# A kernel with its order written out: warm-up matmuls that read the rows of tiles 1 to 3, tile 0 ahead of the others, and a new order on every engine

## The chip, the cores and the metric

The kernel runs on one core of a Trainium2 chip. The core has four compute engines that run side by side: TensorE (PE; its weight loads, PEld, overlap its matmuls), VectorE (DVE), ScalarE (ACT) and GpSimd (POOL), and SyncE (SP), whose queue issues most transfers. Each engine works through its own queue in order and waits on semaphores for the others. The metric is the time of one execution on the device in microseconds (us), as the median of several runs.

## The reference

Inputs are `A_q`, `A_k`, `A_v` of 2048 rows by 640 channels, a short filter, a long filter per channel, and three weight matrices. All are bf16.

```python
xn = _layernorm(A_q)                       # per row, over 640 channels
# branch A: a short filter over 4 rows of k, times v, then a causal convolution with 2048 taps per channel
kv = k_shift * v                           # k_shift[n] = sum over t < 4 of k[n - t] * shift_k[:, t]
y  = irfft(rfft(kv, 4096) * rfft(ssm_k, 4096))[:2048] + kv * ssm_D
A  = xn * y
# branch B: a gated linear unit
g = xn @ w_gate; u = xn @ w_up             # 640 -> 1728
B = (sigmoid(g) * u) @ w_down              # 1728 -> 640
out = A_q + A + B
```

## The kernel before

The 2048 rows lie in 16 tiles of 128 rows, in one buffer `acc` that also collects the output. Four tiles make a group (`tr` 0 to 3).

For branch B, a group is normalised (`rec_stat`, `rec_fast` or `rec_rsq`, `rec_norm`), transposed into `xnT` (group 0 by TensorE and PSUM in `rec_tp`, the others by a transposing transfer), and projected in 14 chunks of 128 columns: five matmuls of 128x512 each for the gate and for the up projection (`rec_fc`, line 774). ScalarE takes the sigmoid (line 736), VectorE multiplies it with the up projection (line 738) into `hT`. Then `rec_down` (line 790) multiplies `hT` with `w_down` in two halves of seven matmuls for each output tile and half of its columns, and VectorE adds the result to `acc` (line 801). The last tile is cut into columns of 320, 240 and 80. Projections and down projections share two PSUM accumulators of one bank (tag `g`).

The first two chunks of group 0 are computed tile by tile as the tiles become ready (`rec_first`, line 753, narrow matmuls of 128x128 and 128x256 into PSUM tiles `c0_0` and `c0_1`), so that work can start before all four tiles are there.

Branch A replaces the convolution by matmuls with tables in ten steps (`idx` 0 to 9). `rec_kv` makes the short filter and its product with v on VectorE (lines 484 to 491, into `kvt`), `rec_st1` (line 510), `rec_st2` (line 530) and `rec_st3` (line 578) are the stages on TensorE, `rec_prod` (lines 552 to 564) the spectral product on VectorE, and `rec_st4` (line 610) the last stage, whose result is multiplied with xn and added to `acc`. Stage results leave PSUM through ScalarE or VectorE (`ev`, lines 329 to 333).

At the start, TensorE runs nine matmuls of zeros on the tile `warm` (line 819, planned at line 820) and, behind the normalised tile 0, one more (line 849). Their result in `wps` is never read.

```python
    for m0, m1 in ((0, 1), (1, 4)):
        for q in range(4):
            load_x(q, m0, m1, "ACT" if q > 1 else "SP", FIX)
```

These loads bring tile 0 and tiles 1 to 3, each in four pieces of 32 partitions, on two queues.

Nothing is scheduled at run time. Each call of `plan.op` records an operation with what it reads and writes. The list `ORDER` (line 79) names the recorded operations by number in the order in which they are emitted, and so fixes the order on every engine and in every queue. `ON_DVE` names the PSUM evacuations that VectorE takes; ScalarE takes the others. The figures for durations and for transfers (`few` in `load_x`) are for a planner that made `ORDER`; they are not used when the kernel is built.

Of the kernel before, what the change touches and what calls it, by code (L numbers as in the profile page):

```python
# [44 lines left out]
def _dft_tables():  # L45
# [31 lines left out]


ORDER = [
# [38 lines left out]
]  # L118
ON_DVE = [
    98, 102, 104, 139, 140, 142, 147, 148, 195, 248, 380, 397, 424, 445, 446, 470, 480, 486, 498, 504, 605  # L120
]


# [94 lines left out]
def kernel(  # L218
# [146 lines left out]

    def load_x(q, m0, m1, eng, pri):
        dma(lambda e: e.dma_start(acc[32 * q:32 * q + 32, m0:m1, :], xq4[q][:, m0:m1, :]), 32, 1280 * (m1 - m0), q=eng,
            few=1.0 if m0 == 0 else 1.2 if m0 == 1 else 2.4, w=[("acc", m, q) for m in range(m0, m1)], pri=pri)

    def weight(tr, n):  # L370
        tr = 0 if tr == 1 else tr
# [264 lines left out]
    def rec_stat(m, pri):  # L636
        b = f"bs{m}"
        ak = [("acc", m, q) for q in range(4)]
        for s2 in range(2):
            dve(320, 1, lambda s2=s2: nc.vector.bn_stats(tl[b][:, 6 * s2:6 * s2 + 6], acc[:, m, s2 * 320:(s2 + 1) * 320]),  # L640
                r=ak, w=[(b, s2)], alloc=[(b, "bs")] if s2 == 0 else (), pri=pri)
        dve(8, 1, lambda: nc.vector.bn_aggr(st[:, 0:2, m], tl[b].rearrange("p (a c) -> p a c", a=2)),
            r=[(b, 0), (b, 1)], w=[("mv", m)], pri=pri)

# [71 lines left out]
    def rec_evac(tr, fc, cs, pri):  # L716
        two = isinstance(cs, str)
        pk = lambda i: (cs, i) if two else (cs[i],)
        pv = lambda i: tl[cs][:, i] if two else tl[cs[i]][:]
        hk = "hT"  # L720
        last = fc == NFC - 1
        sg = f"sig{tr}_{fc}"
        if last:
            c = cs[0]
            act(512, lambda: nc.scalar.activation(tl[sg][64:P, :], tl[c][0:64, :], ACT.Sigmoid),
                r=[(c,)], w=[(sg,)], alloc=[(sg, "sig")], pri=pri - 2000)
            dve(512, 1, lambda: nc.vector.tensor_tensor(hT[64:P, fc, :], tl[sg][64:P, :], tl[c][64:P, :], ALU.mult),
                r=[(c,), (sg,)], w=[(hk, fc)], pri=pri - 2000)
        elif fc in PRM["UP"] and PRM["UP0"] <= pri < PRM["UP1"]:
            act(512, lambda: nc.scalar.activation(tl[sg][:], pv(0), ACT.Sigmoid),  # L730
                r=[pk(0)], w=[(sg,)], alloc=[(sg, "sig")], pri=pri - 2000)
            ev(512, lambda: hT[:, fc, :], lambda: pv(1), r=[pk(1)], w=[(hk, fc), (hk, fc, 0)], pri=pri - 2000)
            dve(512, 2, lambda: nc.vector.tensor_tensor(hT[:, fc, :], tl[sg][:], hT[:, fc, :], ALU.mult),
                r=[(sg,), (hk, fc, 0)], w=[(hk, fc)], pri=pri - 2000)
        else:
            act(512, lambda: nc.scalar.activation(tl[sg][:], pv(0), ACT.Sigmoid),  # L736
                r=[pk(0)], w=[(sg,)], alloc=[(sg, "sig")], pri=pri - 2000)
            dve(512, 1, lambda: nc.vector.tensor_tensor(hT[:, fc, :], tl[sg][:], pv(1), ALU.mult),  # L738
                r=[pk(1), (sg,)], w=[(hk, fc)], pri=pri - 2000)

# [105 lines left out]
    rec_fast(3, FIX + 50, 1.0 / DM)  # L846
    rec_norm(0, FIX + 5, True)
    rec_tp(0, FIX, True)
    plan.op({"PE": (0.43, lambda: warm(1))}, r=[("warm",), ("xn0", 0)], w=[("wps", 1)], pri=FIX + 0.5)
    for m0, m1, k in ((4, 8, "LS1"), (8, NQ, "LNS")):  # L850
        if m0 == 4:
            for m in range(m0, m1):
# [77 lines left out]
```

## Time and profile before

| | us |
|---|---|
| median of 3 runs | 244.5 |
| the 3 runs | 244.73, 243.32, 244.5 |
| profiled execution | 244.61 |
| its span, from first to last instruction | 242.8 |
| mean granted TensorE clock | 0.989 |

A row of a timeline gives the start in us from the span's start, the duration in us, the engine, the line of the kernel, the operation, what it writes and reads with shapes, the number of instructions that are merged, and in brackets the idle time before it with what ended it. Matmuls overlap, so a single one lasts longer than its share of a row. Groups of instructions have the count, then busy us and the mean duration in ns. A row of a stretch gives its limits and length and the busy us of each engine. The granted clock is the share of TensorE's full clock that the throttle let through.

### The profile page before, as it was taken

What the parts mean: (1) busy time and instruction counts of PE and PEld (TensorE: products, weight loads), DVE (VectorE), ACT (ScalarE), POOL (GpSimd) and SP (SyncE); (2) the same over time, 40 slices, a digit from 0 to 9 for tenths busy, and PEclk for the clock granted to TensorE, in tenths of its full rate; (3) what the DMA queues carried; (4) which work ended last, traced back from release to release, by engine and by line L of the source; (5) the groups of instructions that cost most, each with busy time, mean ns of one, the idle gap of its engine ahead of it and who ended that gap; (6) DMA issues with size and microseconds to landing.
All of it is one profiled execution on the core that took longest, in us unless ns stands there. A gap on an engine that the chain in (4) does not pass through costs nothing. (4 is left out here: it accounts for less than half of the span.)

```text
span 242.8 us, 8236 instructions
## 1 busy us (share of the span) xinstructions
PE 230.0 (95%) x3649; PEld 139.3 (57%) x3676; DVE 195.3 (80%) x278; ACT 153.4 (63%) x216; POOL 0.7 (0%) x6
## 2 busy tenths in 40 slices
PE   6699999999999999999999999999999999989891
PEld 1564455775444567675555554777765655456671
DVE  3724577297889898999898999999899499878961
ACT  2713235004799999789988999777689863443320
POOL 1000000000000000000000000000000000000000
PEclk9799999999999999999999999999999999999998
DMA  6999959799988599999997979584443896120591
GB/s 185 313 241 318 160 156 201 200 194 253 158 147 144 135 139 165 219 239 129 237 189 181 287 169 262 122 239 123 121 103 108 222 307 197 55 86 3 153 284 55
DMA packets 92599, 43.72 MB, mean 180 GB/s; under 512 B 69716, under 2 KB 88980, under 8 KB 92308
## 3 DMA queue, kind: packets, MB, share of 16 engines
q1 hardware_dynamic: 92372, 42.87, 76.9%
q8 instruction: 28, 0.46, 0.8%
q10 hardware_dynamic: 192, 0.33, 0.4%
q14 instruction: 7, 0.06, 0.1%
HBM read 30.74 MB, written 5.24 MB: 148 GB/s over the span
## 5 line engine op out<-in xcount | busy, mean ns | idle before, releaser
L774 PE MATMUL g<-xnT,w 128*128 128x512 bf16 x358 | 85.9, 379 | 1.6 <-issue 0.6
L790 PE MATMUL g<-wd,hT 128*128 128x320 bf16 (+2 forms) x462 | 64.5, 295 | 0.7 <-DVE acc L801 0.7
L774 PEld LDWEIGHTS <-w 128*128 128x128 bf16 x380 | 35.3, 98 | 39.1 <-issue 0.8
L790 PEld LDWEIGHTS <-hT 128*128 128x128 bf16 x462 | 43.1, 98 | 16.9 <-issue 0.6
L736 ACT ACTIVATE sig<-g 128x512 bf16<-128x512 f32 x44 | 26.5, 603 | 32.5 <-PE g L774 30.2
L738 DVE TENSOR_TENSOR hT<-sig,g 128x512 bf16<-128x512 bf16 x44 | 30.2, 687 | 20.2 <-PE g L774 17.4
L329 ACT CAST S<-c 128x1024 bf16<-128x1024 f32 (+2 forms) x39 | 37.5, 999 | 10.6 <-PE c L610 5.4
L774 PE MATMUL g<-xnT,VV 128*128 128x512 bf16 x135 | 31.4, 379 | 0.3
L484 DVE TENSOR_TENSOR P<-kt,sT 128x2048 bf16<-128x2048 bf16 x20 | 24.4, 1222 | 0.2
L332 ACT ACTIVATE T<-c 128x1024 bf16<-128x1024 f32 x20 | 19.8, 1027 | 5.4 <-PE c L510 5.4
L801 DVE TENSOR_TENSOR acc<-g,acc 128x320 bf16<-128x320 f32 (+2 forms) x33 | 15.7, 477 | 8.8 <-PE g L790 8.6
L530 PEld LDWEIGHTS <-Mt 64*128 64x128 f16 x1280 | 19.7, 95 | 5.0 <-issue 4.6
L774 PEld LDWEIGHTS <-VV 128*128 128x128 bf16 x140 | 13.4, 98 | 15.6 <-issue 0.2
L329 ACT CAST T<-c 128x1024 bf16<-128x1024 f32 (+1 forms) x20 | 19.6, 1021 | 4.2 <-PE c L610 3.5
L530 PE MATMUL c<-T,Mt 64*128 64x64 bf16 x1280 | 22.0, 190 | 0.0
L329 ACT CAST VV<-c 128x1024 bf16<-128x1024 f32 x18 | 17.9, 1018 | 4.0 <-PE c L578 3.9
L552 DVE TENSOR_TENSOR P<-S,P 128x2048 bf16<-128x2048 bf16 x10 | 12.2, 1219 | 0.6 <-DMA P<-S 0.6
L564 DVE TENSOR_TENSOR S<-P 64x2048 bf16<-64x2048 bf16 x10 | 12.2, 1223 | 0.3
L562 DVE TENSOR_TENSOR S<-S 64x2048 bf16<-64x2048 bf16 x10 | 12.2, 1221 | 0.3
L559 DVE TENSOR_TENSOR S<-S 128x2048 bf16<-128x2048 bf16 x10 | 12.2, 1223 | 0.2
L488 DVE TENSOR_TENSOR P<-P,P 128x2048 bf16<-128x2048 bf16 x10 | 12.2, 1221 | 0.2
L491 DVE TENSOR_TENSOR kvt<-P,vt 128x1024 bf16<-128x1024 bf16 x10 | 11.6, 1158 | 0.0
(73 smaller groups left out, 173.5 us busy)
## 6 DMA issues: line engine op xcount, KB each, us to landing
P<-S SPq DMA_DIRECT2D x20, 256.0 KB, 5.3
w<-in_B_w_gate_dram SPq DMA_DIRECT2D x7, 640.0 KB, 6.7
w<-in_B_w_up_dram SPq DMA_DIRECT2D x7, 640.0 KB, 5.6
kt<-in_A_k_dram SPq DMA_DIRECT2D x8, 320.0 KB, 8.3
xnd<-VV SPq DMA_DIRECT2D x4, 640.0 KB, 4.4
vt<-in_A_v_dram SPq DMA_DIRECT2D x8, 320.0 KB, 7.7
VV<-in_A_ssm_k_dram SPq DMA_DIRECT2D x16, 96.0 KB, 4.6
wd<-in_B_w_down_dram SPq DMA_DIRECT2D x3, 480.0 KB, 4.2
```

The source lines that it names most:

```text
L329: fa = lambda: nc.scalar.copy(out=out_fn(), in_=in_fn())
L332: fa = lambda: nc.scalar.activation(out_fn(), in_fn(), ACT.Copy, scale=scale)
L484: dve(2048, 2, lambda: nc.vector.tensor_tensor(tl[c].rearrange("p i (n c) -> p i n c", c=CJ), two(t), sh(t), ALU.mult), r=kr + [("s",)], w ...
L488: dve(2048, 2, lambda: nc.vector.tensor_tensor(tl[a][:], tl[a][:], tl[b][:], ALU.add), r=[(b,)], w=[(a,)], pri=pri)
L530: nc.tensor.matmul(tl[c][:, b, 64 * kk:64 * kk + 64], lhsT=Mb[rows, (k + 16 * b) % 32, 64 - 64 * r:192 - 64 * r], rhs=tl[T][rows, 2 * k + ...
L552: dve(n, 2, lambda: nc.vector.tensor_tensor(Q(), X(), Q(), ALU.mult), r=[(Z, "h", 0), (Z, "h", 1)], w=[(Z, 0)], pri=pri)
L559: dve(n, 2, lambda: nc.vector.tensor_tensor(X(), X(), H(), ALU.mult), r=[(Z, 0)] + sr, w=[(S_, "p")], pri=pri + 0.01)
L736: act(512, lambda: nc.scalar.activation(tl[sg][:], pv(0), ACT.Sigmoid), r=[pk(0)], w=[(sg,)], alloc=[(sg, "sig")], pri=pri - 2000)
L738: dve(512, 1, lambda: nc.vector.tensor_tensor(hT[:, fc, :], tl[sg][:], pv(1), ALU.mult), r=[pk(1), (sg,)], w=[(hk, fc)], pri=pri - 2000)
L774: nc.tensor.matmul(tl[c][:], lhsT=w()[:, k, o:o + P], rhs=tl[X][:, k, :], start=(k == 0), stop=(k == NC - 1))
L790: nc.tensor.matmul(tl[pd[i]][:, 0:d1 - d0], lhsT=hT[:, fc, t4 * P:(t4 + 1) * P], rhs=wd[:, fc, d0:d1], start=(fc == 0), stop=(fc == NFC - 1))
L801: dve(d1 - d0, 1, lambda i=i, m=m, pd=pd, d0=d0, d1=d1: nc.vector.tensor_tensor(acc[:, m, d0:d1], tl[pd[i]][:, 0:d1 - d0], acc[:, m, d0:d1 ...
```

## The change

Five things change.

- Warm-up: the single matmul behind the normalised tile 0 is replaced by two, which wait for the statistics of tile 0 alone. Five new ones stand behind the transposes of tile 0. They move rows of tiles 1, 2 and 3 of `acc` through the array, and so wait for all pieces of these tiles. Their result isn't read either.
- The statistics of tile 1 are recorded as reading tile 0's reciprocal, so that they come behind it on VectorE. The new order also issues both pieces of tile 0 in each queue ahead of those of tiles 1 to 3, where SyncE's and ScalarE's queues had them mixed or turned round.
- The sigmoid of a chunk whose two projections share one PSUM tile (the two chunks of `rec_first`) is recorded as reading both projections.
- The planner's transfer figures for `load_x` change. They have no effect on the built program but through `ORDER`.
- `ORDER` and `ON_DVE` are new throughout. `ON_DVE` still has 21 entries.

In the new order, group 0's wide projections begin with chunks 3 and 2, in place of 7, 4 and 5; the second halves of the first weight blocks are issued ahead of the second blocks. The memset of `Dt` and the load of `ssm_D` that waits for it come early. At the end, the last tile's columns are computed in the order 320, first half of 240, 80, second half of 240, in place of 240, 320, 80, and stored in the order 320, 80, 240.

```diff
 ORDER = [
-    1, 0, 5, 8, 10, 4, 7, 6, 12, 3, 11, 9, 72, 73, 74, 77, 78, 75, 76, 79, 87, 88, 92, 97, 13, 15, 80, 81, 93, 99, 89,
...
+    1, 0, 5, 7, 6, 8, 4, 9, 11, 10, 12, 3, 72, 73, 74, 105, 75, 76, 13, 15, 61, 14, 87, 88, 2, 64, 92, 77, 78, 79, 82,
...
 ON_DVE = [
-    98, 102, 104, 139, 140, 142, 147, 148, 195, 248, 380, 397, 424, 445, 446, 470, 480, 486, 498, 504, 605
+    34, 100, 102, 139, 140, 145, 146, 183, 196, 198, 223, 239, 300, 410, 425, 441, 446, 471, 481, 499, 808
 ]
...
         dma(lambda e: e.dma_start(acc[32 * q:32 * q + 32, m0:m1, :], xq4[q][:, m0:m1, :]), 32, 1280 * (m1 - m0), q=eng,
-            few=1.0 if m0 == 0 else 1.2 if m0 == 1 else 2.4, w=[("acc", m, q) for m in range(m0, m1)], pri=pri)
+            few=1.0 if m0 == 0 else 2.0 if m0 == 1 else 1.9, w=[("acc", m, q) for m in range(m0, m1)], pri=pri)
...
             dve(320, 1, lambda s2=s2: nc.vector.bn_stats(tl[b][:, 6 * s2:6 * s2 + 6], acc[:, m, s2 * 320:(s2 + 1) * 320]),
-                r=ak, w=[(b, s2)], alloc=[(b, "bs")] if s2 == 0 else (), pri=pri)
+                r=ak + ([("rs", 0)] if m == 1 else []), w=[(b, s2)], alloc=[(b, "bs")] if s2 == 0 else (), pri=pri)
...
             act(512, lambda: nc.scalar.activation(tl[sg][:], pv(0), ACT.Sigmoid),
-                r=[pk(0)], w=[(sg,)], alloc=[(sg, "sig")], pri=pri - 2000)
+                r=[pk(0)] + ([pk(1)] if two else []), w=[(sg,)], alloc=[(sg, "sig")], pri=pri - 2000)
...
-    plan.op({"PE": (0.43, lambda: warm(1))}, r=[("warm",), ("xn0", 0)], w=[("wps", 1)], pri=FIX + 0.5)
+    plan.op({"PE": (0.86, lambda: warm(2))}, r=[("warm",), ("mv", 0)], w=[("wps", 1)], pri=FIX + 0.5)
+    def warm_x():
+        for i in range(5):
+            nc.tensor.matmul(tl["wps"][:, 0, 0:512], lhsT=tl["warm"][:, 0:P], rhs=acc[:, 1 + i % 3, 0:512], start=True, stop=True)
+    plan.op({"PE": (1.07, warm_x)}, r=[("warm",), ("pst0_0", 0)] + [("acc", m, q) for m in range(1, 4) for q in range(4)],
+            w=[("wps", 2)], pri=FIX + 0.5)
```

74 rows, old and new, of the table ORDER are left out of this document.

## The prediction

> **What bounds the kernel now.** I read the page first, then the waits of TensorE, then the busy time of stretches, then the timelines of TensorE, VectorE and ScalarE in the first 15 us, and those of the end.
>
> ```profile
> span 242.8 us, 8236 instructions
> ```
>
> ```profile
> PE g L790 <- DVE acc L801: 0.7, 1, 0.7
> PE g L774 <- issue: 0.6, 4, 0.2
> PE c L610 <- issue: 0.6, 1, 0.6
> ```
>
> The waits above are those behind 14.42 us (total, times, longest). In the stretches below stand length, busy time of PE, PEld, DVE, ACT and POOL, granted clock, DMA share and GB/s.
>
> ```profile
> 5.55:8.97 3.42, 0.87 (x11) 0.68 (x12) 2.52 (x9) 2.54 (x8) 0.00 (x0) 1.00 1.02 314
> 8.97:12.38 3.41, 3.39 (x31) 3.03 (x29) 1.89 (x7) 2.27 (x3) 0.00 (x0) 0.50 1.10 309
> 14.42:237.10 222.68, 219.25 (x3559) 132.08 (x3584) 187.20 (x252) 147.13 (x204) 0.00 (x0) 1.00 0.79 179
> 237.10:242.80 5.70, 0.47 (x13) 0.33 (x10) 0.73 (x2) 0.00 (x0) 0.00 (x0) 0.85 0.18 50
> 100.00:150.00 50.00, 49.16 (x913) 29.58 (x921) 47.48 (x54) 45.10 (x55) 0.00 (x0) 1.00 0.96 211
> ```
>
> TensorE is the bound: from 14.42 us, where the wide projections begin, to 237.10 it is idle for 222.68 - 219.25 = 3.43 us in all. So there are three places where time can be had: the 14.42 us ahead of the wide projections, those 3.43 us, and the 5.70 us behind the last full tile. The start is the largest. In it the granted clock falls to half for one stretch of 3.41 us, right behind a stretch of the same length in which TensorE was busy for 0.87 us. The step by step of it:
>
> ```profile
> 1.22 4.02 PE L819 MATMUL c<-sig 128*128 128x512 bf16 x9 [1.22 <-DVE sig L808]
> 7.86 0.45 PE L706 MATMUL g<-VV 128*128 128x128 bf16 x5 [2.62 <-DVE VV L684]
> 8.56 0.45 PE L706 MATMUL g<-VV 128*128 128x128 bf16 x5 [0.24 <-DVE VV L684]
> 8.85 0.48 PE L819 MATMUL c<-sig 128*128 128x512 bf16 x1
> 9.35 3.28 PE L753 MATMUL c<-xnT,VV 128*128 128x128 bf16 x30
> 12.46 0.72 PE L706 MATMUL g<-VV 128*128 128x128 bf16 x10
> 13.02 1.56 PE L753 MATMUL c<-xnT,VV 128*128 128x128 bf16 x25
> 14.42 6.64 PE L774 MATMUL g<-xnT,VV 128*128 128x512 bf16 x29
> ```
>
> ```profile
> 5.12 0.21 DVE L642 BATCH_NORM_AGGREGATE st<-bs 128x2 f32<-128x12 f32 x1
> 6.36 0.89 DVE L640 BATCH_NORM_STATS2 bs<-acc 128x6 f32<-128x320 bf16 x2 [1.03 <-DMA acc<-in_A_q_dram]
> 7.16 0.15 DVE L660 RECIPROCAL st<-st 128x1 f32<-128x1 f32 x1
> 7.28 0.21 DVE L642 BATCH_NORM_AGGREGATE st<-bs 128x2 f32<-128x12 f32 x1
> 7.41 0.39 DVE L684 TENSOR_SCALAR VV<-acc,st 128x640 bf16<-128x640 bf16 x1
> 7.86 0.16 DVE L660 RECIPROCAL st<-st 128x1 f32<-128x1 f32 x1
> 8.05 0.45 DVE L684 TENSOR_SCALAR VV<-acc,st 128x640 bf16<-128x640 bf16 x1
> ...
> 10.50 0.45 DVE L684 TENSOR_SCALAR VV<-acc,st 128x640 bf16<-128x640 bf16 x1
> ```
>
> ```profile
> 5.36 0.29 ACT L658 ACTIVATE st<-st 128x1 f32<-128x1 f32 x1 [1.48 <-DVE st L642]
> 6.31 0.74 ACT L647 ACTIVATE VV<-acc 128x640 bf16<-128x640 bf16 x1 [0.65 <-DMA acc<-in_A_q_dram]
> ...
> 7.53 0.29 ACT L658 ACTIVATE st<-st 128x1 f32<-128x1 f32 x1 [0.16 <-DVE st L642]
> ...
> 9.05 0.69 ACT L329 COPY xnT<-g 128x640 bf16<-128x640 bf16 x1
> ```
>
> The variance of tile 0 is there at 5.33 and its square root at 5.65, but the reciprocal runs at 7.16: ahead of it VectorE holds the statistics of tile 1, whose rows land at 6.36. This is the 2.6 us wait of the first transposes. Then 30 narrow matmuls take 3.28 us (109 ns each) at half clock; 25 later ones take 1.56 (62 ns each) at full clock. Tiles 2 and 3 were normalised by 10.95 (10.50 + 0.45), yet their transposes stand behind those 30 and run only at about 12.5.
>
> **Part 1, the start.** The new order puts tile 0's reciprocal and normalisation ahead of tile 1's statistics. From 5.65: reciprocal 0.15, a small memset, normalisation 0.39, so tile 0's transposes start at about 6.4 in place of 7.86. Two warm-up matmuls start at 5.4, when tile 0's statistics are done, and at 0.43 each (nine took 4.02) and faster once the clock is granted they end by 6.2, in time that was idle; the one at 8.85 goes. The five new matmuls on rows of tiles 1 to 3 wait for the transposes (6.85) and for rows that were there at 6.31 and 6.36, and take 5 x 0.229 (29 in 6.64) = 1.15 us, to 8.0. Behind them stand tile 1's transposes, which wait for tile 1's normalisation in any case: its statistics still begin at 6.36, and its square root still sits behind tile 3's sum on ScalarE (7.53), so about 8.6 as before. The added matmuls cost nothing as long as the rows land before 7.4; each us of later landing past that would push the chain by a us. From 9.05 twenty narrow matmuls at 62 ns take 1.25 and ten more 0.62, to 10.9. ScalarE now copies tile 0's transposed rows (0.69) ahead of tile 3's squares, which puts tile 3 at about 11.05; its transposes end near 11.4, twenty more narrow matmuls end at 12.65, and the first wide projection starts there: 14.42 - 12.65 = 1.77 us sooner. Before it 50 narrow matmuls have run in place of 55, so 5 x 0.062 = 0.31 is still owed. Gain: **1.46 us, if the clock holds.** If it falls as before, thirty narrow ones at 109 ns last from 9.05 to 12.3, the transposes to about 12.9 and the twenty others to 14.1, which with the 0.31 leaves nothing.
>
> Does it hold? In the stretch 5.55 to 8.97 TensorE was busy for 0.87 us, and would now be busy for about 0.35 + 0.45 + 1.15 + 0.4 = 2.35. The trace has one stretch with 0.87 (clock lost) and one with 3.39 (clock granted behind it), so 2.35 lies nearer to the holding side.
>
> The Trainium skill ("TensorE: Matmul & The Clock Gate", Part 1) says that a window of some 3.4 us that runs freely decides, and that an idle window brings half rate; the 3.41 us stretch at 0.50 agrees. The same page (Part 4) says that transposes do not count as busy in the same way, which speaks against the change; no row here shows it. Its result is the second rival's.
>
> **Part 2, the loads.** The start is also close to the DMA's limit (share 1.02 and 1.10 in the first two stretches above). Starting TensorE sooner does not bring the loads sooner. The wide projections come 1.77 us sooner, and the new order begins them with the second half of the first two weight blocks, which it also issues ahead of the blocks that came first until now. Now 29 of them run without a gap (6.64 us), so none waits for a weight; I cost this at nothing, and if supply sets their start after all, the 1.46 are lost and nothing beyond. The other place where supply can bite is the first convolution step that needs A_v:
>
> ```profile
> 74.11 1.15 DVE L491 TENSOR_TENSOR kvt<-P,vt 128x1024 bf16<-128x1024 bf16 x1
> ```
>
> ```profile
> 76.44 0.41 PE L510 MATMUL c<-Ft,kvt 32*128 32x64 f16 x32
> ```
>
> ```profile
> 64.21 2.03 SPq L443 DMA_DIRECT2D vt<-in_A_v_dram  x1
> ```
>
> ```profile
> vt<-in_A_v_dram SPq DMA_DIRECT2D x8, 320.0 KB, 7.7
> ```
>
> The last of these is the median from issue to landing of the A_v loads. By the order of the two programs, ten wide matmuls (10 x 0.229 = 2.3 us) that stood ahead of this step now stand behind it, so TensorE arrives at 76.44 - 1.46 - 2.3 = 72.7. The product was ready at 75.26. If that stays, 2.56 us are lost; if the product follows its load directly (64.21 + 7.7 = 71.9, plus 1.15 = 73.06), 0.4. VectorE's order now has fewer of the later chunks' multiplies right ahead of the product, so I take 0.4, near the load's own row, and keep 0 to 2.56.
>
> **Part 3, the middle.** The set of 21 evacuations that VectorE takes is another, of the same number, and all engines carry the same work. Of the 3.43 us, the 0.7 at L790 comes from the second half of tile 12's down projection waiting for VectorE; in the new order seven matmuls of tile 12 stand between the partial sum and the reuse of its buffer. I take 0.4 as gained, with -0.7 to +2 as bounds: +2 is the order of one new wait of each size that the list above shows. The wait at L610 for the evacuation of the step before stays: one projection stands between the two in both orders. The sigmoids of the first two chunks wait for the second projection as well; their products on VectorE needed that anyway, so this costs nothing.
>
> **Part 4, the end.**
>
> ```profile
> 235.20 0.41 DVE L801 TENSOR_TENSOR acc<-g,acc 128x240 bf16<-128x240 f32 x1 [0.62 <-PE g L790]
> 237.10 0.74 DVE L801 TENSOR_TENSOR acc<-g,acc 128x320 bf16<-128x320 f32 x2 [1.49 <-PE g L790]
> ```
>
> ```profile
> 238.21 1.22 SPq L627 DMA_DIRECT2D out_dram<-acc  x2
> ```
>
> TensorE ends at 237.57 (0.47 busy behind 237.10). Two additions and two store issues of 0.61 each follow, and the last issue starts at 238.82, 1.25 later. In the new order the last matmuls are those of the 240 columns; the 320 and the 80 are added and issued before, so one addition (0.41) and its signals stand before the last issue, about 0.6. Gain 0.6; the last store is three times as wide, so I keep -0.7 to +0.2.
>
> **The sum.** -1.46 + 0.4 - 0.4 - 0.6 = -2.06. The profiled execution took 244.61 (span 242.8 and 1.81 around it), so 242.55; it lies 0.11 above the median of 244.5, so 242.45 against the median. I say 242.5.
>
> **The rivals.** *The clock falls anyway:* part 1 gives nothing in place of 1.46: 243.9. For it: without the transposes the stretch would hold only 1.5 busy us. Against it: that is still more than the 0.87 that lost it. *The loads take it back:* the 2.56 at the first product in place of 0.4: 244.6. For it: the DMA share above; against it: VectorE, not the load, held the product. *VectorE becomes the bound, slower:* in 100 to 150 us VectorE is busy for 47.48 of 50, 95%. Projections have two accumulators, freed by VectorE in the order written out; where one of the products (1.15 to 1.22 us) or two stand ahead of a release, TensorE waits for them. There are ten convolution steps; four such waits of 1.15 bring 4.6 and 247.1, and from two on the gain is gone. For it: 95%; against it: the present order has the same load and loses 3.43 in all.
>
> **Chances.** Forecast 0.56, clock 0.15, loads 0.15, VectorE 0.14. The forecast alone spans 241.2 to 243.8: the end and the middle at their bounds. The range to 245.6 takes in the first two rivals and the near part of the third; what lies outside is most of the slower case and a small part below 241. A measurement of this kernel tells about 1%, 2.4 us, from no change: half of the forecast's case lies under 242.05 (0.28), the rest of it and the two middle rivals within (0.58), the third above (0.14).
>
> **What would show it.** Granted clock near 1.00 from about 5.5 us on, no stretch at 0.50 ahead of the wide projections; tile 0's transposes at 6.4; the first L774 at 12.7; a wait of under 1 us ahead of the first L510 that reads kvt; idle TensorE of some 3 us between there and the last tile; the last store issued 0.6 us behind the last matmul. The prediction is wrong if the clock drops in the start, if the first kvt step waits 2 us or more, or if TensorE's idle time in the middle exceeds 5 us.

## The result and the profile after

| | before | after |
|---|---|---|
| median, us (6 runs each) | 244.1 | 241.45 |
| profiled execution, us | 244.61 | 241.67 |
| its span, us | 242.8 | 239.0 |
| mean granted clock | 0.989 | 0.997 |

The ratio of after to before is 0.9891 (95% interval 0.9861 to 0.992): 2.65 us less, 1.1%. On another chip the same pair gave 0.9867 (0.9836 to 0.9899). The forecast was 242.5, and the time lies inside its range of 241.0 to 245.6, 1.05 below the number. One of after's six runs took 247.18; it counts in the median and not in the ratio.

TensorE's timeline at the start of after, with the same columns as before:

```profile
1.22 4.51 PE L819 MATMUL c<-sig 128*128 128x512 bf16 x11 [1.22 <-DVE sig L808]
5.61 0.45 PE L706 MATMUL g<-VV 128*128 128x128 bf16 x5
5.90 1.24 PE L852 MATMUL c<-acc,sig 128*128 128x512 bf16 x5
8.01 0.45 PE L706 MATMUL g<-VV 128*128 128x128 bf16 x5 [0.87 <-DVE VV L684]
8.30 1.84 PE L753 MATMUL c<-xnT,VV 128*128 128x128 bf16 x30
9.97 0.72 PE L706 MATMUL g<-VV 128*128 128x128 bf16 x10
10.53 1.28 PE L753 MATMUL c<-xnT,VV 128*128 128x128 bf16 x20
11.65 1.24 PE L774 MATMUL g<-xnT,VV 128*128 128x512 bf16 x4
```

The reader is to see three things. The wait of 2.62 us ahead of tile 0's transposes is gone (7.86 has become 5.61). The thirty narrow matmuls take 1.84 us in place of 3.28, so they run at full clock. The first wide projection starts at 11.65 in place of 14.42. The stretches of after, with the columns of the stretches before (length, busy time of PE, PEld, DVE, ACT and POOL, granted clock, DMA share, GB/s):

```profile
5.22:8.63 3.41, 2.54 (x24) 1.31 (x22) 3.08 (x10) 2.73 (x7) 0.00 (x0) 1.00 1.12 318
8.63:12.05 3.42, 3.40 (x58) 3.22 (x57) 1.85 (x6) 1.78 (x4) 0.00 (x0) 1.00 1.03 320
```

```profile
11.65:233.84 222.19, 219.85 (x3570) 132.52 (x3596) 189.00 (x253) 148.32 (x204) 0.00 (x0) 1.00 0.82 183
233.84:238.90 5.06, 0.02 (x1) 0.00 (x0) 0.41 (x1) 0.00 (x0) 0.00 (x0) 0.84 0.15 40
```

The clock is granted from 5.22 on and stays until the work ends. Behind the first wide projection TensorE is idle for 222.19 - 219.85 = 2.34 us, where it was 3.43. What it waits for (total, times, longest):

```profile
PE g L706 <- DVE VV L684: 0.9, 1, 0.9
PE c L610 <- issue: 0.5, 1, 0.5
PE g L774 <- issue: 0.2, 1, 0.2
```

The 0.7 at L790 has gone, and no wait for VectorE has come in its place.

Where the span's 3.80 us went: the first wide projection comes 2.77 sooner, but 0.15 more work stands behind it (219.87 busy to the end of TensorE in place of 219.72); 1.09 less idle time in the middle; and the part behind TensorE's last matmul is 5.14 in place of 5.23, 0.09 less. Together 2.77 - 0.15 + 1.09 + 0.09 = 3.80. Around the span lie 2.67 us in place of 1.81, so the execution's time fell by 2.94 only. In other profiled executions of this study that remainder was between 1.8 and 3.0 us, in no relation to the kernel; it isn't explained here.

### The profile page after: what moved, and what is told of

Read it like the earlier page. It is cut to its first block, busy times and chain, and to the rows that moved or that the text cites. A ratio compares the mean times of both kernels' runs of the same rounds, so it can differ in the third digit from the quotient of the medians.

```text
span 239.0 us, 8246 instructions
## 1 busy us (share of the span) xinstructions
PE 229.4 (96%) x3653; PEld 138.3 (58%) x3682; DVE 196.7 (82%) x278; ACT 154.0 (64%) x216; POOL 0.7 (0%) x6
## 4 chain that ended last, share of the span: by engine, by line
PE 93%; DMA 1%; issue 1%; DVE 1%; ACT 1%; ACTq 1%; DVEq 0%
PE g L774 46%; PE g L790 26%; PE c L530 9%; PE c L578 4%; PE c L510 3%; PE c L610 2%; PE c L753 2%; DMA acc<-in_A_q_dram 1%; ACT T L329 1%; DVE bs L640 1%; ACTq L367 1%; PE g L706 0%; ACT sig L736 0%; DVE VV L684 0%; DVE acc L801 0%
## 5 line engine op out<-in xcount | busy, mean ns | idle before, releaser
L774 PE MATMUL g<-xnT,w 128*128 128x512 bf16 x357 | 86.2, 379 | 1.2 <-issue 0.2
L790 PE MATMUL g<-wd,hT 128*128 128x320 bf16 (+2 forms) x462 | 65.1, 295 | 0.0
L774 PEld LDWEIGHTS <-w 128*128 128x128 bf16 x380 | 35.3, 98 | 38.8
L790 PEld LDWEIGHTS <-hT 128*128 128x128 bf16 x462 | 42.9, 98 | 16.7
L329 ACT CAST S<-c 128x1024 bf16<-128x1024 f32 (+2 forms) x38 | 36.5, 1004 | 9.0 <-PE c L530 5.5
L774 PE MATMUL g<-xnT,VV 128*128 128x512 bf16 x134 | 31.7, 379 | 0.3
L329 ACT CAST T<-c 128x1024 bf16<-128x1024 f32 (+1 forms) x22 | 21.5, 1018 | 4.6 <-PE c L510 2.6
L774 PEld LDWEIGHTS <-VV 128*128 128x128 bf16 x140 | 13.3, 98 | 15.5 <-issue 0.2
L332 ACT ACTIVATE T<-c 128x1024 bf16<-128x1024 f32 x19 | 19.0, 1026 | 1.7 <-PE c L510 1.5
L329 ACT CAST VV<-c 128x1024 bf16<-128x1024 f32 x16 | 15.8, 1017 | 1.9 <-PE c L578 1.6
```

The source lines that it names most:

```text
L329: fa = lambda: nc.scalar.copy(out=out_fn(), in_=in_fn())
L332: fa = lambda: nc.scalar.activation(out_fn(), in_fn(), ACT.Copy, scale=scale)
L774: nc.tensor.matmul(tl[c][:], lhsT=w()[:, k, o:o + P], rhs=tl[X][:, k, :], start=(k == 0), stop=(k == NC - 1))
L790: nc.tensor.matmul(tl[pd[i]][:, 0:d1 - d0], lhsT=hT[:, fc, t4 * P:(t4 + 1) * P], rhs=wd[:, fc, d0:d1], start=(fc == 0), stop=(fc == NFC - 1))
```

## The experiments

The theory was the prediction's: the start gives most, by tile 0 first and by a clock that the added warm-up holds. The rivals: the gain is in the order of the rest; the warm-up has no part in it; and, for the small gain at the end, what sets that end.

### The start alone, and the rest alone

```diff
 ORDER = [                # start_only: after's order up to the last projection of group 0, then before's order
-    ... after's order behind group 0's projections
+    ... before's order of the same operations
 ]
-                r=[pk(0)] + ([pk(1)] if two else []), w=[(sg,)], alloc=[(sg, "sig")], pri=pri - 2000)
+                r=[pk(0)], w=[(sg,)], alloc=[(sg, "sig")], pri=pri - 2000)
```

```diff
 ORDER = [                # rest_only: the kernel before, with after's order behind group 0's projections
-    ... before's order behind group 0's projections
+    ... after's order of the same operations
 ]
```

> The new order up to the last projection of group 0 (first 44 us), the old order behind it. If the start earned the gain (2.4 us there, half of it the clock that no longer falls), about 241.8 against 244.1 of the kernel before. If the new order behind the start earned it and the start's lead is lost again to the loads, about 243.8.

Measured: 241.55 against 243.99, ratio 0.9894 (0.9859 to 0.9929).

> The old start, with one warm-up matmul and none on rows of tiles 1 to 3, and the new order behind the projections of group 0. If the start earned the gain, about 243.4: the 0.66 us wait for tile 12's buffer goes and little else. If the new order behind the start earned it, about 241.7.

Measured: 243.15 against the same 243.99, ratio 0.9964 (0.994 to 0.9989). The start is worth 1.06%, about 2.6 us, the rest 0.36%, about 0.9 us. Together that is more than the 1.09% of the whole change (1.33% on the other chip), but the intervals allow it. The execution of start_only that was profiled had been disturbed (597 us), so its trace isn't read, and the kernel was run once more for a trace:

> The new order up to the last projection of group 0 and the old one behind it, for its trace: the first wide projection at 11.7 as in the changed kernel, no stretch at 0.50, and the 0.66 us wait for tile 12's buffer and idle time of about 3.4 us in all behind it, as in the kernel before.

Measured: one execution of 242.1, span 240.3, the clock granted from 5.97 on, the first wide projection at 11.87. What TensorE waits for in it, of the waits that aren't in after:

```profile
PE g L774 <- DVE hT L727: 1.2, 1, 1.2
...
PE g L790 <- DVE acc L801: 0.7, 1, 0.7
PE g L774 <- issue: 0.6, 4, 0.2
```

This is where the rest of the order earns its part: with after's start and before's order behind it, the 0.7 at L790 and the 0.6 of issue are there again. The wait of 1.2 for a product stands at the seam of the two orders; neither before nor after has it, so it is a price of this mixture. In rest_only, with before's start, TensorE is idle for 2.41 us behind the first wide projection, as in after.

### The five matmuls, and all of the added warm-up

```diff
-        for i in range(5):
+        for i in range(0):
```

> The changed kernel without the five matmuls on rows of tiles 1 to 3; the two others stay. If those five hold the clock, it falls to 0.50 for one stretch of 3.4 us ahead of the wide projections, the thirty narrow matmuls take 109 ns each again, and the time is about 1.4 us over the changed kernel, 242.9. If tile 0's earlier work alone holds the clock, 241.4 and no stretch at 0.50.

Measured: 240.94 against 243.99, ratio 0.9885 (0.9844 to 0.9925). The expectation missed: without the five the median is as low as with them. Five runs of the seventeen of this kernel (here and in its repetition below) lie above 242.5, up to 245.05, and one of eleven of the changed kernel. Those five have a mean granted clock of 0.981 to 0.993, eleven of the other twelve 0.998 or more, which fits a clock that was lost in the start; no trace of them shows it. The next kernel leaves out the two matmuls behind tile 0's statistics too:

```diff
-    plan.op({"PE": (0.86, lambda: warm(2))}, r=[("warm",), ("mv", 0)], w=[("wps", 1)], pri=FIX + 0.5)
+    plan.op({"PE": (0.86, lambda: warm(0))}, r=[("warm",), ("mv", 0)], w=[("wps", 1)], pri=FIX + 0.5)
...
-        for i in range(5):
+        for i in range(0):
```

> The changed kernel without the two and without the five warm-up matmuls; nine remain, and the order is the same. If TensorE's busy time in a stretch of 3.4 us decides on the clock, it is about 1.3 us here and the clock falls in many runs: 242.9 where it falls, 241.4 where it doesn't, median between. If tile 0's place alone holds it, 241.4 throughout.

Measured: 243.49 against 244.56, ratio 0.9952 (0.9921 to 0.9984). Its timeline of TensorE, from tile 1's transposes on:

```profile
7.91 0.45 PE L706 MATMUL g<-VV 128*128 128x128 bf16 x5 [1.76 <-DVE VV L684]
8.20 2.67 PE L753 MATMUL c<-xnT,VV 128*128 128x128 bf16 x30
...
13.18 1.24 PE L774 MATMUL g<-xnT,VV 128*128 128x512 bf16 x4
```

The clock in the stretch that holds most of the narrow matmuls:

```profile
8.99:12.40 3.41, 3.41 (x36) 3.41 (x34) 1.40 (x5) 0.45 (x2) 0.00 (x0) 0.50 1.07 312
```

The narrow matmuls start at 8.20, no later than in after; all that is lost is the clock, and the wide projections start 1.53 us later (13.18 against 11.65). Because a few tenths were in dispute, the kernel without the five was timed again beside the changed one, on one chip:

> The changed kernel once more, as the mark for the other three on this chip. Expected at 0.989 of the kernel before (95% interval of the first measurement 0.986 to 0.992), the clock granted throughout.

Measured: 241.38 against 244.65, ratio 0.9867 (0.9836 to 0.9899).

> The changed kernel without the five matmuls on rows of tiles 1 to 3, timed beside the changed kernel on one chip. Theory A, the five decide whether the clock holds: without them the stretch after the first grant holds some 1.5 to 1.8 us of work, close to the value between 1.55 (lost) and 1.58 (held), so a good part of the runs loses the clock and the median is 0.5 us or more above the changed kernel's, single runs up to 1.5 us above. Rival B, the two matmuls behind tile 0's statistics suffice: the medians agree within 0.3 us.

Measured: 241.14 against the same 244.65, ratio 0.9865 (0.9825 to 0.9906), runs from 240.69 to 245.05. Rival B holds for the median: the two matmuls suffice. Whether the five make the rare slow starts rarer can't be told from so few runs. The part of the change that is its most conspicuous, rows of tiles 1 to 3 moved through the array, brings nothing to the median that these runs can measure.

### The warm-up without tile 0 first, tile 0 first without the warm-up, and both

```diff
 ORDER = [                # before_warm: 105 are the two matmuls, 106 the five, in place of the single one (105 in before)
-    1, 0, 5, 8, 10, 4, 7, 6, 12, 3, 11, 9, 72, 73, 74, 77, 78, 75, 76, 79, 87, 88, 92, 97, 13, 15, 80, 81, 93, 99, 89,
+    1, 0, 5, 8, 10, 4, 7, 6, 12, 3, 11, 9, 72, 73, 74, 105, 77, 78, 75, 76, 79, 87, 88, 92, 97, 106, 13, 15, 80, 81,
...
```

```diff
 ORDER = [                # before_tile0: pieces of tile 0 (5 to 8) first, tile 1's statistics (77, 78) behind tile 0
-    1, 0, 5, 8, 10, 4, 7, 6, 12, 3, 11, 9, 72, 73, 74, 77, 78, 75, 76, 79, 87, 88, 92, 97, 13, 15, 80, 81, 93, 99, 89,
+    1, 0, 5, 7, 6, 8, 9, 11, 10, 12, 4, 3, 72, 73, 74, 75, 76, 87, 88, 92, 77, 78, 79, 97, 13, 15, 80, 81, 93, 99, 89,
...
```

```diff
 ORDER = [                # tile0_warm: both
-    1, 0, 5, 8, 10, 4, 7, 6, 12, 3, 11, 9, 72, 73, 74, 77, 78, 75, 76, 79, 87, 88, 92, 97, 13, 15, 80, 81, 93, 99, 89,
+    1, 0, 5, 7, 6, 8, 9, 11, 10, 12, 4, 3, 72, 73, 74, 105, 75, 76, 87, 88, 92, 77, 78, 79, 97, 106, 13, 15, 80, 81,
...
```

> The kernel before in its own order, with the two and the five new warm-up matmuls in place of the single one. If the clock is what counts, it stays granted: the narrow matmuls take 62 ns, 1.4 us less, and 0.6 of it is given back because the five now stand between the transposes of tiles 0 and 1 when tile 1 is ready: about 243.3. If tile 0's place in the queues is what counts, no gain: 244.1 or slower by the 0.6.

Measured: 243.91 against 243.99, ratio 0.9994 (0.9962 to 1.0027), runs from 242.06 to 245.87. The one that was profiled took 242.24 and held the clock, with the first wide projection at 12.61. With tile 1's statistics still in front, tile 0's transposes run at 7.17 only, and the stretch behind the first grant holds 1.57 us of TensorE's work, the least of all that kept the clock (below). Of its twelve runs the five slowest (244.33 to 245.87) have the five lowest mean clocks, 0.988 to 0.993, where the profiled one has 0.999. That fits a lost clock, but no trace of them shows it.

> The kernel before with three moves in its order: both pieces of tile 0 first in each queue, and tile 1's statistics behind tile 0's normalisation; its single warm-up matmul stays. Tile 0's transposes start at about 5.7 in place of 7.9. If the clock is half of the start's gain, it still falls here and the time is 243.3 to 243.6. If tile 0's place is all of it, 241.7.

Measured: 243.78 against 244.56, ratio 0.9981 (0.9955 to 1.0006). Tile 0's transposes run at 5.64, as in after, and nearly nothing comes of it. Its timeline of TensorE:

```profile
8.73 3.36 PE L753 MATMUL c<-xnT,VV 128*128 128x128 bf16 x30
...
13.91 1.46 PE L774 MATMUL g<-xnT,VV 128*128 128x512 bf16 x5
```

The time that was won ahead of tile 1 doesn't reach the narrow matmuls. They start at 8.73, right behind VectorE's copy of the transposed rows (8.21 to 8.68), and in rest_only, which has before's start, at 8.82. Then they run at half clock (3.36 us).

> The kernel before with two of the parts alone: tile 0's pieces and its statistics first, and the two plus five warm-up matmuls; all else in the order of before. Theory A, these two together hold the clock and bring the narrow matmuls forward, which is the gain of the start: tile 0 first alone gave 0.46, the clock is worth 1.5, so 2.0 us below the kernel before (ratio 0.992). Rival B, the rest of the new start (order of the weight blocks, the copies, the chunks) is needed: 0.5 us or less below (0.998), the first wide projection no earlier than 12.6.

Measured: 242.95 against 244.65, ratio 0.9946 (0.9912 to 0.998), that is 1.3 us less (0.5 to 2.2). In its trace the clock holds and the first wide projection starts at 12.44. That is sooner than rival B allowed; in time it lies midway between the two theories, and the interval takes in both. Neither part alone gives a gain that can be told from none (0.06% and 0.19%); both together give 0.54%, four tenths of the 1.33% of the whole change on this chip. That the two are worth more together than singly is within the intervals and so isn't shown by the times.

The traces part the start's gain better, from one execution each (times in us):

| kernel | clock | narrow matmuls from | first wide projection |
|---|---|---|---|
| rest_only (start of before) | lost | 8.82 | 14.07 |
| before_tile0 | lost | 8.73 | 13.91 |
| before_warm | held | 8.82 | 12.61 |
| tile0_warm | held | 8.82 | 12.44 |
| no_extra_warm (start of after without the added warm-up) | lost | 8.20 | 13.18 |
| after | held | 8.30 | 11.65 |

The first wide projection of rest_only, before_warm and tile0_warm:

```profile
14.07 1.24 PE L774 MATMUL g<-xnT,VV 128*128 128x512 bf16 x4
```

```profile
12.61 2.75 PE L774 MATMUL g<-xnT,VV 128*128 128x512 bf16 x11
```

```profile
12.44 2.75 PE L774 MATMUL g<-xnT,VV 128*128 128x512 bf16 x11
```

With the added warm-up, and the clock that it holds, the wide projections come 1.46, 1.47 and 1.53 us sooner. Tile 0 first gives 0.16 and 0.17, and the rest of the start's order 0.73 and 0.79. In that rest only 50 narrow matmuls stand ahead of the wide ones in place of 55, and they no longer wait as in tile0_warm,

```profile
8.82 1.83 PE L753 MATMUL c<-xnT,VV 128*128 128x128 bf16 x30 [0.34 <-DVE xnT L330]
```

where the copy of the transposed rows is late. So most of the start's gain is the clock, and tile 0 first by itself is next to nothing. What it may add is that the clock holds in more of the runs: the stretch behind the first grant has 3.05 busy us in tile0_warm against 1.57 in before_warm, and none of its nine runs has a mean clock under 0.994, where five of before_warm's twelve have. Two traces don't show that.

### The end

After's end, by SyncE's queue and VectorE's last addition:

```profile
222.46 10.98 SPq L631 DMA_DIRECT2D out_dram<-acc  x12
233.53 1.97 SPq L627 DMA_DIRECT2D out_dram<-acc  x3
```

```profile
233.90 0.41 DVE L801 TENSOR_TENSOR acc<-g,acc 128x240 bf16<-128x240 f32 x1 [0.48 <-PE g L790]
```

The last three stores are issued back to back from 233.53 to 235.50, while the sum of the 320 columns was ready at 232.4 and the last one at 234.31. The stores of tile 14 hold the queue until 233.4, so the last issue starts at 234.96, 1.10 behind the last matmul. If the queue is what is late, fewer issues on it should help. In the first try two of the last three stores go to ScalarE's queue:

```diff
-                2 * (d1 - d0) * (m1 - m0), few=3.0, r=key, w=[("out", m0, d0)], pri=pri)
+                2 * (d1 - d0) * (m1 - m0), few=3.0, q="SP" if d0 == 560 else "ACT", r=key, w=[("out", m0, d0)], pri=pri)
```

> The changed kernel with the stores of the last tile's 320 and 240 columns issued from ScalarE's queue, which is empty by then; the one of 80 columns and all others stay on SyncE's. If SyncE's issuing of one store after the other (0.6 to 0.7 us each) is what kept the end from getting shorter, the last issue starts 0.5 us behind the last matmul in place of 1.1, and the time is 0.5 under the changed kernel. If the landing of all stores sets the end, no change.

Measured: 243.15 against 244.56, ratio 0.9951 (0.9925 to 0.9978): slower than after. Of SyncE's waits from 220 us on, the one that is new:

```profile
SPq L631 <- DMA out_dram<-acc: 2.5, 1, 2.5
```

A piece of tile 14 in SyncE's queue now waits 2.5 us for the landing of an earlier store: in the built program the transfers use a few completion semaphores in turn, whichever queue issues them, and a store may only go out when the one that had its semaphore before has landed. So this run put a new wait in place of the old one and decides nothing on the question. Nor is the wait all of the difference in the traces: of the 3.3 us by which the span is longer than after's, 2.2 lie ahead of TensorE's last matmul (236.02 against 233.86), with waits for transfers of 0.5 and 0.8 us at 110 and 129 us, long before the changed stores. That part isn't explained. In the second try tile 14 is stored by one transfer:

```diff
-                LS1=55.48, LNS=70.0, EVB=-0.5, ST4=2.0, GP=2, H0=22.227, B0=79.117, SP=30.34, ML=15,
+                LS1=55.48, LNS=70.0, EVB=-0.5, ST4=2.0, GP=2, H0=22.227, B0=79.117, SP=30.34, ML=14,
```

> The changed kernel with tile 14 stored by one transfer in place of four, so that SyncE issues four stores at the end in place of seven. Theory A, the back-to-back issues of SyncE set the end: three issues of 0.42 to 0.72 us fall away, the queue is free when the last addition (0.41 us) ends, the last issue starts 0.5 to 0.6 us behind the last matmul in place of 1.10, and the time is 0.5 us below the changed kernel's. Rival B, the last addition and its signals set it: no change within 0.2 us.

Measured: 243.02 against 244.65, ratio 0.9942 (0.9915 to 0.9969), 1.6 us slower than after on the same chip. In its trace the last matmul ends at 234.35 and the last issue starts at 234.83, 0.48 behind it, as theory A said; but the span ends at 240.5, 6.1 behind the last matmul in place of 5.1. SyncE's waits from 229 us on for landed stores, of this kernel and then of after:

```profile
SPq L930 <- DMA out_dram<-acc: 4.0, 1, 4.0
```

```profile
SPq L930 <- DMA out_dram<-acc: 2.2, 2, 1.3
```

and one stretch behind the last issue, of this kernel and then of after (the last two numbers are the DMA share and GB/s):

```profile
236.00:238.00 2.00, 0.00 (x0) 0.00 (x0) 0.00 (x0) 0.00 (x0) 0.00 (x0) 0.59 0.24 68
```

```profile
236.00:238.00 2.00, 0.00 (x0) 0.00 (x0) 0.00 (x0) 0.00 (x0) 0.00 (x0) 0.83 0.15 38
```

Both theories had the issue as the last thing. It isn't: with the last issue as early as in after (234.83 against 234.96) SyncE waits 1.8 us longer for stores to land, and in the stretch from 236 to 238 more is still being moved (68 GB/s against 38). The landing of the stores ends this kernel. About 1.0 of the profiled difference is there; the other 0.5 is ahead of it (TensorE ends at 234.35 in place of 233.86); half of that is there at the first wide projection already (11.91 against 11.65), and the rest isn't explained. The packets in the two traces show what the longer landing is: the 128 rows of tile 14 move from 233.08 to 236.78 in the one transfer, in after's four from 232.69 to 234.26. The last tile's rows stand behind them and end at 238.80 in place of 237.04. Why the one transfer moves its rows more slowly wasn't tried. So this run doesn't show either what an earlier last issue would bring if nothing else changed.

## Why the prediction was right, and where its terms were off

**The whole.** The time fell into the range, and the mechanism of the largest term was right: the clock is granted all through. The prediction's two cases for the first wide projection, 12.65 with the clock and 14.1 without, lie 1.45 apart, and the traces put the clock at 1.46 to 1.53. Tile 0's reciprocal ahead of tile 1's statistics, which heads that term, is worth 0.2 by itself. The sum of -2.06 became -2.94 in the profiled execution, with errors in both directions in it; that they cancel in part is luck.

**Part 1, -1.46, measured -2.62** (2.77 less the 0.15 behind it). The step that went wrong is the times at which rows land, which I took from the trace of before. VectorE's statistics of tile 0 and 1 in after:

```profile
3.41 0.89 DVE L640 BATCH_NORM_STATS2 bs<-acc 128x6 f32<-128x320 bf16 x2 [1.64 <-DMA acc<-in_A_q_dram]
...
5.11 0.45 DVE L684 TENSOR_SCALAR VV<-acc,st 128x640 bf16<-128x640 bf16 x1
5.75 0.89 DVE L640 BATCH_NORM_STATS2 bs<-acc 128x6 f32<-128x320 bf16 x2 [0.19 <-DMA acc<-in_A_q_dram]
```

Tile 0's rows are there at 3.41, and in before_tile0, which has only the order of the pieces and of the statistics changed, at 3.44; in before, rest_only and before_warm, without that order, at 4.20, 4.23 and 4.09. I had named this order in the description and given it no price; tile 0's rows come 0.8 sooner by it, but the chain doesn't hang on them. It hangs on tile 1's rows, which I left at 6.36 and which come at 5.75; but in rest_only and before_warm, with the order of before, they come at 5.83 and 5.67, so the 6.36 was one late execution, and I had built the chain to 12.65 on it. With tile 1's transposes at 8.01 in place of 8.6 and the narrow matmuls at 8.30 in place of 9.05 the first wide projection moves by the same 0.75. The rest of the difference of 1.0 is in the main tile 3, which I had reckoned late by ScalarE's copy: in after its transposes follow the thirty narrow matmuls without a wait. The work still owed was 0.15 in place of 0.31. The late rows also flatter the measured number: rest_only, with the same start as before, has its first wide projection at 14.07, so some 0.35 of the 2.77 belongs to that one execution of before.

**Does the clock hold.** It did, and the comparison of 0.87 busy us before with an estimated 2.35 (2.54 measured) pointed the right way. What held it isn't what I had counted on alone: without the five matmuls, worth 1.15 in my sum, it holds in both executions that were profiled. And the 0.87 was misread, as the last section shows: it was all transposes. Where the prediction says "Its result is the second rival's", the first rival is meant, the clock that falls.

**Part 2, +0.4, measured 0.** The sentence "Starting TensorE sooner does not bring the loads sooner" failed. SyncE's queue in before, and then in after:

```profile
42.28 0.40 SPq L693 DMA_DIRECT2D xnd<-VV  x1
...
54.29 9.88 SPq L443 DMA_DIRECT2D vt<-in_A_v_dram  x3
```

```profile
39.78 0.39 SPq L693 DMA_DIRECT2D xnd<-VV  x1
...
50.75 11.94 SPq L443 DMA_DIRECT2D vt<-in_A_v_dram  x4
```

Ahead of A_v stand transfers that wait for results, as the store of normalised rows; they went 2.50 us sooner, and A_v behind them 3.54. The start alone does most of this: A_v is issued at 51.10 in start_again and at 53.50 in rest_only. VectorE's product and the first step that reads it, in after:

```profile
70.47 2.25 DVE L491 TENSOR_TENSOR kvt<-P,vt 128x1024 bf16<-128x1024 bf16 x2
```

```profile
71.83 0.41 PE L510 MATMUL c<-Ft,kvt 32*128 32x64 f16 x32
```

TensorE arrives at 71.83, sooner than my 72.7, and the product is there at about 71.6. No wait is left, so the rival that the loads take it back is out too.

**Part 3, -0.4, measured -1.09.** The 0.7 at L790 went, as named, and the list of waits has no new one; the 0.6 of issue at L774 fell to 0.2. By rest_only this comes with the new order and not with the start. VectorE is busy for 189.00 of 222.19 us, 85%, and the list of waits behind the first wide projection shows no wait of TensorE for it: the rival that ended on the slower side is out.

**Part 4, -0.6, measured -0.09.** I had the last issue 0.6 behind the last matmul by the addition in front of it, and it is 1.10 behind: I had counted the two additions and not the issues of tile 14's four pieces and of the last tile's first two stores, which stand back to back in the queue ahead of it. The step was also wrong in kind: what ends the kernel is the landing of the stores, for which SyncE waits 2.2 us at the end of after, 1.8 in before and 4.0 in tail_one, and which the sum took as the same.

**The other rivals.** The clock falls anyway: in no_extra_warm it does, and then 1.1 us of the gain are left (0.5%), where I had computed 0.6. By the bound of about 1% that I set, the measured 1.1% lies just on the faster side, to which I had given 0.28.

## What to carry to other kernels

Price the landings ahead of the first instruction as carefully as the instructions behind them, ask which of them the chain hangs on, and take them from more than one execution: here one late landing of 0.5 to 0.7 us went into the sum. Where parts of a change act through one another, read each part's share from the traces by the same event, here the first wide projection; the medians of single parts, 0.06% and 0.19%, told nothing. At the end of a kernel, read what follows the last issue before moving the issue.

## What the runs showed of the hardware

The granted clock changes on a grid of 3.41 us whose start differs between executions: the first grant came at 3.95 us in one (no_warm_x_again) and at 7.10 in another (tile0_warm). Ahead of it the rows show 1.00 too, though nine matmuls of 128x512 take 4.02 us there, 0.45 each, against 0.229 later: the trace has no record of that time, and a run's mean clock leaves it out. In the 13 traces with a record of the clock it fell, if at all ahead of the end of the work, one stretch of 3.41 us behind the first grant. That first stretch in four executions: before and rest_only, which lost the clock behind it, then before_warm and no_warm_x, which held it. The second number is TensorE's busy time:

```profile
5.58:8.99 3.41, 0.89 (x11) 0.68 (x12) 2.54 (x9) 2.51 (x8) 0.00 (x0) 1.00 1.03 314
```

```profile
5.83:9.24 3.41, 1.54 (x19) 1.10 (x20) 3.32 (x12) 3.07 (x8) 0.00 (x0) 1.00 1.07 347
```

```profile
4.42:7.83 3.41, 1.57 (x11) 0.69 (x10) 2.84 (x11) 2.32 (x7) 0.00 (x0) 1.00 1.00 283
```

```profile
6.26:9.67 3.41, 1.77 (x32) 1.60 (x30) 3.25 (x12) 2.81 (x9) 0.00 (x0) 1.00 1.08 308
```

Two more lost it, with 1.16 (before_tile0) and 1.53 (no_extra_warm); no_warm_x_again held it with 1.60, and all others with 2.29 or more. So 1.54 busy us of 3.41 lost the clock and 1.57 held it (the 1.55 and 1.58 of the expectation above): a boundary so narrow, between executions of different kernels, that it may be chance, the more so as the ends of matmuls are modelled. The Trainium skill ("TensorE: Matmul & The Clock Gate", Part 1) brings half rate behind an idle window of this length; here windows with up to 1.54 us of work brought it.

The same page (Part 4) says that transposes don't count as busy in the same way, and on this the rows of before say more than I had read in them. The transposes alone in that stretch (L706, busy time of TensorE), in before, rest_only, before_warm and no_warm_x:

```profile
5.58:8.99 3.41, 0.89 (x10) 1.00 1.03 314
```

```profile
5.83:9.24 3.41, 0.91 (x10) 1.00 1.07 347
```

```profile
4.42:7.83 3.41, 0.45 (x5) 1.00 1.00 283
```

```profile
6.26:9.67 3.41, 0.71 (x9) 1.00 1.08 308
```

The 0.89 us of before were all transposes. Without them rest_only, which lost the clock, had 1.54 - 0.91 = 0.63 us of other work, and before_warm and no_warm_x, which held it, 1.57 - 0.45 = 1.12 and 1.77 - 0.71 = 1.06. That parts the two sides by 0.43 in place of 0.03 (no_extra_warm and before_tile0 had 0.91 of transposes too and lie below 0.63), and so the trace speaks for the page's rule; no run here tried transposes by themselves, and it stays open. If it holds, the two matmuls behind tile 0's statistics count for their full time in that stretch, and the ten transposes for nothing.
